# The start of a linear-attention block on one core: the last piece of a modulation matrix split between VectorE and TensorE, with new instruction orders

## The chip, the cores and the metric

The kernel runs on one core of a Trainium2 chip. A core has TensorE (PE, with its weight loads shown apart as PEld), VectorE (DVE), ScalarE (ACT), GpSimd (POOL) and SyncE (SP), which issues most DMAs. Each engine works through its own queue in order. The metric is the device time of one execution in microseconds; 2048 tokens of width 576 go through an attention block and an MLP.

## The reference

```python
mod = (silu(c) @ w_mod).reshape(1, 6, 1, 576)          # c: 1 x 576, w_mod: 576 x 3456
sa, ca, ga, sb, cb, gb = ...                           # six rows of mod
h = layernorm(x) * (1 + ca) + sa
q, k, v = heads of h @ wqkv                            # 32 heads of 18
phi = lambda t: where(t > 0, t + 1, exp(t)) + 1e-6
num = phi(q) @ (phi(k)^T v);  den = phi(q) . sum(phi(k))
x = x + ga * ((num / den) @ wo)
h = layernorm(x) * (1 + cb) + sb
x = x + gb * (silu(h @ w1) @ w2)                       # w1: 576 x 4608, w2: 4608 x 576
```

Everything is float32 outside. Inside, most products are made with operands split into a rounded high part and a low part that holds the rest, so one product becomes three passes: high by high, high by low, low by high.

## The kernel before, in words

The width 576 is cut into four chunks of 128 rows and a tail of 64 (KC = 4, START = 0..4; the tail stands twice, in both halves of a 128-row chunk). Tokens come in tiles of 128 and blocks of 512.

The start, which the change rewrites, makes two columns for each chunk: sa, the shift (a = 0), and 1 + ca, the scale (a = 1). w_mod's first 1152 columns come in five pieces by rows: four full ones in `mods[0..3]` (the tile is named hT in the trace) and the tail in `tmod`. VectorE multiplies piece 0 by its part of silu(c) (`sc`, line L583) and adds pieces 1 and 2 with theirs (L586), all into piece 0, called `rows`. What then remains is a sum over the 128 partitions: TensorE does it by one-column products (L522) with a chunk of 128 columns of `rows` as weights and a column of ones as the moving operand. The last piece goes by one-column products with `sc` itself as the moving column; the tail by products with two columns (`sel`, L519). All of these accumulate in one place of PSUM, `colp`, and `add_cols` (L526) copies them out, adding 1 to the scales. ScalarE copies the last 64 columns to stand twice (L589).

Meanwhile x tiles 0 and 1 are normalised (L355 makes the offset that ScalarE's normalising needs, L361 is ScalarE's and L363 VectorE's), turned by TensorE into PSUM (L531), and when the columns are there each chunk becomes a feature: `modulate` on VectorE (L371) or ScalarE (L369), then `split_h` rounds it (L375 on ScalarE) and takes the rest (L271 on VectorE). The k weights are rounded by `w_hi` (L476) and their rests taken by `w_lo` (L481, for the tail L483). `first_k` then makes the first real products (L548) of tiles 0 and 1 for chunks 0 to 3, and `k_part` the others. While TensorE has nothing else it multiplies ones by ones: `keep_busy(n)` issues n such fillers (L542), whose result nobody reads.

Later, project (L861) makes q and k of all tiles in two PSUM rooms named psK, used in turn. Each is read by ScalarE (L868) and VectorE (L874) before it is written again. `sum_steps` (L986) adds phi(k)^T h of each block. LayerNorm statistics are L346 (BN_STATS) and L347. Transposes of the normed q by DMA (L1368) feed the attention output (L399), and scans of the MLP weights (L661, squares by ScalarE, L662) give scale factors; then comes the MLP (L1935 up, L2019 down).

The order on each engine is not that of the source. `arrange(ORDERS, begun)` (L2390) takes a table of numbers per engine, found by a search outside the kernel, and chains the instructions of that engine in that order; what the table doesn't name keeps its place behind. So an engine waits for each of its instructions in the table's order, whatever is ready behind it.

Of the kernel before, what the change touches and what calls it, by code (L numbers as in the profile page):

```python
# [18 lines left out]
P = 128  # L19
# [5 lines left out]
def kernel(ctx: ExitStack, tc, A_x, A_wqkv, A_wo, B_x, B_w1, B_w2, c, w_mod, out):  # L25
# [33 lines left out]
    def behind(instructions):  # L59

        with ExitStack() as order:
# [7 lines left out]
            0-12 22 18-19 27-31 13-16 23-24 17 20-21 25-26 37-56 32-36 57-60 63-64 61-62 65-66 69-70 67-68 71-78 81-82  # L69
            85-86 79-80 89-93 96-97 83-84 87-88 94-95 98-117 126 118-121 127 122 128-133 123-124 134-135 125 136-137  # L70
            156-159 138-139 160-161 140-151 162-163 152-155 164-181 184-191 320-321 192-197 182-183 198-201 296
            202-217 297 218-223 322-325 224-235 326-327 298-299 236-239 328-331 300-301 240-245 302-303 246-251
            304-305 252-257 268-269 258-263 270-277 306-307 332-337 278-281 338-341 308-309 342-343 310-317 264-265
            318-319 282-293 368-369 266-267 370-373 294-295 344-345 374-375 346-351 376-377 352-355 378-381 356-365
            408-409 366-367 410-411 436-439 382-387 392-397 412-417 398-405 440-441 388-389 418-423 390-391 424-429
            442-443 406-407 430-435 444-479 492-495 480-483 496-499 484-485 500-501 486-491 502-505 600-601 506-509
            576-579 510-511 520-527 512-517 528-529 580-585 530-531 518-519 602-615 586-587 532-535 548-551 616-617
            552-555 588-591 556-557 592-593 536-537 618-621 558-569 594-599 622-623 538-543 570-571 624-629 544-547
            630-637 648-649 638-641 650-655 642-647 656-661 572-575 672-675 662-663 676-683 664-669 688-689 716-721
            684-687 670-671 690-693 722-723 694-715 724-739 744-745 740-743 746-761 772-779 880-881 762-767 780-781  # L80
            856-859 768-771 782-791 860-861 792-809 862 810-811 828-841 882-883 812-817 863-865 818-819 884-887
            866-873 888-889 874-879 820-823 842-847 824-827 890-893 904-905 848-851 894-895 852-855 906-909 896-901
            910-915 902-903 916-925 968-969 996-1001 970-983 926-927 1002-1005 984-991 1006-1009 928-931 992-995
            932-935 952-953 1010-1013 954-957 1014-1015 958-961 1016-1023 936-937 1024-1025 938-943 1026-1027 962-963
            1028-1035 964-965 1036-1039 944-945 1052-1059 966-967 1060-1061 946-951 1062-1069 1040-1051 1070-1079
            1137-1138 1080-1103 1108-1109 1139-1142 1110-1113 1143-1146 1104-1105 1114-1115 1106-1107 1147-1148
            1116-1117 1149-1150 1118-1121 1151-1152 1122-1135 1153-1160 1185-1191 1197-1206 1136 1207-1210 1161
            1211-1214 1162-1168 1215-1220 1169-1170 1287-1288 1171-1176 1289-1292 1177-1182 1293-1296 1183-1184 1192
            1245-1250 1193 1297-1298 1221-1238 1251-1252 1239-1244 1253-1256 1194 1257-1260 1195 1261-1263 1196
            1264-1285 1299-1316 1286 1317-1372 1389-1392 1373-1382 1417-1418 1383-1388 1419-1422 1393-1410 1423-1424  # L90
            1411-1416 1425-1430 1445-1456 1431-1444 1473-1482 1457-1458 1501-1502 1459-1460 1503-1506 1461-1462
            1507-1508 1463-1472 1509-1518 1483-1492 1519-1522 1493-1496 1523-1530 1497-1500 1531-1552 1557-1560
            1585-1594 1553-1556 1595-1602 1561-1564 1613 1617-1618 1565-1574 1619 1614-1615 1620 1603-1604 1616
            1629-1638 1575-1584 1605-1608 1639 1621 1625-1626 1609-1612 1622-1624 1627-1628 1640-1646 1661-1662
            1689-1690 1647-1648 1691-1696 1649-1656 1697-1708 1657 1709-1710 1658 1711-1718 1663-1672 1659-1660
            1673-1674 1745-1748 1675-1676 1749-1751 1719-1720 1752 1721 1753-1757 1677-1688 1722 1758-1760 1723-1730
            1761-1768 1731-1741 1773 1742-1744 1769-1772 1785-1788 1813 1774-1775 1814-1816 1829-1830 1789-1796
            1831-1832 1797-1800 1817-1819 1833-1834 1776-1779 1837-1838 1820-1821 1835 1780-1781 1822 1782 1801-1802
            1836 1783-1784 1839 1803-1804 1840 1805-1810 1823 1811-1812 1824-1828 1841-1864 1869-1870 1925 1871-1872
            1865-1868 1926 1873 1885-1886 1874-1877 1939 1878 1913 1927-1928 1914-1915 1879 1887-1888 1940 1929  # L100
            1880-1881 1930 1941-1942 1889-1892 1882 1916-1919 1893-1904 1943-1945 1905-1906 1883-1884 1907-1908
            1931-1932 1909-1912 1933-1936 1953-1958 1920-1921 1959-1964 1937 1965-1970 1938 1922 1946-1948 1923-1924
            1949-1951 1971-1972 1952 1981 1973-1974 1993-1998 1982 1999-2000 1975-1978 2001-2004 1983 2005-2006
            1979-1980 1984-1986 2007-2008 1987-1989 2009-2012 1990-1992 2021 2037-2038 2013-2018 2022-2027 2049-2052
            2019-2020 2053-2059 2039-2040 2060 2028 2061-2068 2029-2030 2069-2070 2031 2041 2071 2032 2042 2072-2074
            2033-2036 2081-2082 2045 2083-2084 2075-2076 2085-2088 2043-2044 2093-2094 2089 2046-2048 2095-2104
            2077-2080 2105-2108 2090 2109-2116 2121-2123 2117-2120 2133 2124-2125 2134-2144 2126 2145-2146 2091-2092
            2127-2132 2147-2149 2151-2152 2150 2153-2158 2165-2168 2159-2164 2173-2174 2183 2175 2184 2176 2193-2195
            2169-2170 2185 2171-2172 2177 2179-2182 2178 2199-2202 2189-2192 2186-2188 2205 2203 2229 2204 2196-2198
            2230 2211 2231-2232 2206 2233 2217-2221 2243 2207 2212-2213 2222 2214 2234 2223-2224 2235 2225-2228  # L110
            2236-2237 2208 2215 2238-2242 2209-2210 2244 2216 2245-2257 2263-2264 2258 2269 2265-2266 2270-2271
            2259-2260 2272 2261 2267-2268 2262 2275-2280 2273-2274 2287-2304 2281-2286 2305 2311-2312 2306-2309 2325
            2310 2326-2329 2313-2314 2330 2315-2324 2331-2347 2355 2367 2348-2354 2361-2363 2368-2371 2379 2372
            2364-2366 2380-2382 2385 2383 2356 2384 2386-2388 2357-2360 2397-2402 2389-2390 2373-2376 2403 2377-2378
            2417-2424 2437-2441 2391-2393 2405 2404 2406-2408 2442 2394 2489 2409 2395 2501 2455-2458 2396 2459-2462
            2502-2506 2475 2411-2412 2410 2413-2415 2476-2478 2490 2479-2481 2425 2482 2426-2430 2416 2491-2494
            2443-2448 2431-2435 2513 2436 2514-2518 2449-2454 2519-2520 2527-2528 2463-2469 2529-2533 2483-2484 2534
            2485-2486 2470-2472 2487-2488 2473-2474 2541-2546 2495-2500 2553-2556 2507-2510 2557-2560 2521-2522
            2511-2512 2523-2524 2567-2572 2535 2573-2574 2525-2526 2536-2540 2581-2585 2547-2549 2561-2566 2586 2593
            2550-2552 2594-2596 2587-2590 2597 2591-2592 2575-2576 2598 2577-2580 2605-2610 2599 2613 2600-2604  # L120
            2614-2615 2611-2612 2616-2618 2627-2632 2619-2623 2639-2640 2624-2625 2641-2642 2626 2673 2653-2656
            2643-2644 2657-2658 2633-2638 2674-2678 2645-2646 2679 2647-2652 2667 2680-2682 2668-2669 2683 2670-2672
            2684-2685 2659-2665 2686 2666 2691 2687 2697 2688-2690 2698-2700 2692-2694 2701-2704 2717-2718 2695-2696
            2719-2724 2709-2710 2725-2726 2705-2708 2711-2713 2727-2728 2714-2716 2729-2734 2755-2756 2807-2808
            2735-2736 2809 2825 2737-2743 2826 2757-2758 2810-2811 2744 2749-2753 2759-2761 2754 2767 2745 2762
            2746-2747 2763 2768-2769 2748 2770-2773 2764-2766 2775-2776 2787 2777 2812 2788-2789 2778 2790 2774
            2779-2782 2791-2792 2795-2799 2783 2863 2793-2794 2800-2802 2864 2784-2785 2865-2866 2786 2803-2806
            2867-2869 2813-2816 2843-2850 2831-2832 2827-2830 2817-2819 2833-2838 2820 2839 2870 2821-2824 2840-2842
            2883-2887 2851-2859 2871-2872 2860-2861 2873 2862 2901-2903 2888 2904-2908 2874-2877 2889-2896 2878-2882
# [2293 lines left out]
```

## Time and profile before

| | us |
|---|---|
| three timed runs | 1068.85, 1073.65, 1073.93 (median 1073.65) |
| the profiled execution | 1067.39 |
| its span in the trace | 1065.7 |
| TensorE busy in the span | 1051.7 (99%) |
| VectorE, ScalarE, GpSimd busy | 872.5, 718.0, 739.7 |
| mean granted TensorE clock | 0.996 |

The profile is of one execution; the timed runs are others. The span begins with the first instruction that the profiler saw. A line such as `L522 PE MATMUL psG<-ones,hT` gives source line, engine, operation, the tile written and the tiles read. In the timeline "x20" counts records, and a float32 product of the program is two records. Text in brackets behind a row is the idle time of that engine before it and what ended it. "Busy" of TensorE includes its waits inside a pipeline and its fillers.

### The profile page before, as it was taken

To read this page: it belongs to the slowest core of one execution; us is meant where nothing else is said; L and a number is where in the kernel's file an instruction comes from. 1 tells how busy PE (TensorE), PEld (TensorE's weight loads), DVE (VectorE), ACT (ScalarE), POOL (GpSimd) and SP (SyncE) were. 2 spreads that over 40 slices of the span, in tenths; PEclk is the share of its full clock that TensorE was granted. 3 is DMA by queue.
4 is the path that set the end of the run, shared out by engine and by line. 5 is a ranking of instruction groups with operands and counts; after the bars stand their busy time and mean duration, and the time that the engine had idled before them with its cause. 6 is when DMAs were issued, how large, how long until landed. Compare 5 with 4: busy or idle time off the path is not lost.

```text
span 1065.7 us, 19010 instructions
## 1 busy us (share of the span) xinstructions
PE 1051.7 (99%) x6981; PEld 742.2 (70%) x6981; DVE 872.5 (82%) x1434; ACT 718.0 (67%) x1343; POOL 739.7 (69%) x808
## 2 busy tenths in 40 slices
PE   8999999999999999999999999999999999999998
PEld 8999999887775565656666666666666666666665
DVE  5876865688999997898988888978977987898757
ACT  5865565458676967776866766767767766776554
POOL 2557446565832888899798678876876878687463
PEclk8999999999999999999999999999999999999999
DMA  9496971294866876587577667657566567526422
GB/s 303 142 205 194 133 203 28 59 214 90 247 173 219 282 219 227 157 279 214 148 239 212 189 205 214 197 202 220 175 217 204 190 199 238 187 89 200 153 81 111
DMA packets 139245, 198.74 MB, mean 186 GB/s; under 512 B 63820, under 2 KB 96464, under 8 KB 139152
## 3 DMA queue, kind: packets, MB, share of 16 engines
q1 hardware_dynamic: 106340, 196.35, 60.2%
q10 hardware_dynamic: 32812, 1.18, 3.2%
q8 instruction: 54, 0.88, 0.4%
q14 instruction: 39, 0.32, 0.1%
HBM read 176.77 MB, written 15.48 MB: 180 GB/s over the span
## 4 chain that ended last, share of the span: by engine, by line
PE 77%; DVE 10%; ACT 4%; DMA 4%; issue 2%; SPq 2%; POOL 1%; DVEq 0%; ACTq 0%; POOLq 0%
PE up L1935 31%; PE down L2019 30%; PE psK L861 5%; PE psG L986 4%; PE big L399 2%; PE big L1451 1%; DVE w L277 1%; PE small L1440 1%; DVE hT L271 1%; DMA hT<-in_w_mod_dram 1%; DMA acc<-turned 1%; DMA qT<-pn 1%; PE psK L548 1%; DMA hT<-hd 1%; DVE st L346 1%
## 5 line engine op out<-in xcount | busy, mean ns | idle before, releaser
L1935 PE MATMUL up<-hT,w 128*128 128x512 f16 x1264 | 319.9, 379 | 0.8 <-DMA hT<-hd 0.8
L1935 PEld LDWEIGHTS <-w 128*128 128x128 f16 x1492 | 145.7, 98 | 133.0 <-DMA hT<-hd 1.9
L2028 DVE SCALAR_TENSOR_TENSOR acc<-acc,set,down 128x576 f32<-128x576 f32 x128 | 103.4, 809 | 31.9 <-PE down L2019 31.2
L1953 ACT ACTIVATE f<-f,set 128x512 f32<-128x512 f32 x102 | 73.3, 718 | 60.1 <-DVE f L1959 50.1
L1973 POOL TENSOR_TENSOR s<-f,f 128x256 f32<-128x256 f32 x66 | 54.7, 828 | 73.4 <-ACT f L1954 70.9
L2019 PE MATMUL down<-w,hb 128*128 128x288 f16 x600 | 91.6, 286 | 0.4 <-DVE U L2030 0.3
L2019 PE MATMUL down<-w,hc 128*128 128x288 f16 x600 | 90.9, 286 | 0.0
L2019 PE MATMUL down<-w,hT 128*128 128x288 f16 x480 | 82.8, 286 | 0.4 <-DVE acc L2032 0.4
L1957 DVE TENSOR_TENSOR f<-up,p 128x512 f32<-128x512 f32 x102 | 69.5, 681 | 16.5 <-PE up L1935 8.6
L1954 ACT ACTIVATE f<-f,set 128x512 f32<-128x512 f32 x102 | 73.6, 721 | 3.0
L2019 PEld LDWEIGHTS <-hb 128*128 128x128 f16 x600 | 58.7, 98 | 24.2 <-issue 1.2
L2019 PEld LDWEIGHTS <-hc 128*128 128x128 f16 x600 | 58.7, 98 | 22.0 <-issue 0.3
L1997 POOL TENSOR_TENSOR hc<-s,hc 128x512 f16<-128x512 f32 x50 | 63.2, 1264 | 7.2 <-ACT hc L1993 7.1
L1959 DVE TENSOR_TENSOR f<-up,f 128x512 f32<-128x512 f32 x68 | 46.7, 687 | 26.2 <-PE up L1935 25.6
L1977 POOL TENSOR_TENSOR f<-f,s 128x256 f32<-128x256 f32 x66 | 53.9, 816 | 19.9 <-DVE hb L1997 12.1
L399 PE MATMUL big<-w,qT 128*128 128x288 f16 x448 | 65.0, 286 | 1.8 <-DMA qT<-pn 0.7
L2019 PEld LDWEIGHTS <-hT 128*128 128x128 f16 x480 | 46.9, 98 | 26.6 <-issue 0.8
L1970 POOL TENSOR_TENSOR s<-f 128x256 f32<-128x256 f32 x66 | 56.4, 854 | 5.4 <-ACT f L1950 3.9
L1975 POOL TENSOR_TENSOR s<-s,f 128x256 f32<-128x256 f32 x66 | 55.8, 845 | 3.3
L2019 PE MATMUL down<-w,ha 128*128 128x288 f16 x396 | 56.8, 286 | 0.0
L2019 PE MATMUL down<-w,hd 128*128 128x288 f16 x396 | 56.5, 286 | 0.0
L986 PE MATMUL psG<-w,xs 128*128 128x288 f32 x336 | 54.8, 295 | 0.0
(420 smaller groups left out, 2765.1 us busy)
## 6 DMA issues: line engine op xcount, KB each, us to landing
hT<-hd SPq DMA_DIRECT2D x101, 640.0 KB, 4.7
hT<-hd SPq DMA_DIRECT2D x65, 512.0 KB, 4.1
hT<-in_B_w_dram SPq DMA_DIRECT2D x14, 576.0 KB, 5.3
hT<-in_B_w_dram SPq DMA_DIRECT2D x28, 256.0 KB, 5.7
raw<-in_B_w_dram SPq DMA_DIRECT2D x11, 576.0 KB, 6.5
v<-in_B_w_dram SPq DMA_DIRECT2D x9, 576.0 KB, 5.3
raw<-in_B_w_dram SPq DMA_DIRECT2D x9, 512.0 KB, 4.9
acc<-in_A_x_dram SPq DMA_DIRECT2D x16, 288.0 KB, 6.2
```

The source lines that it names most:

```text
L399: T.matmul(ps, xpart(a), wpart(b), start=n == 0, stop=n == len(XW) - 1)
L986: T.matmul(ps[:, h, :HALF], l, pk[t][:, u, h * HALF : (h + 1) * HALF], start=t == 0 and m == 0, stop=t == 3 and m == len(left) - 1)
L1935: T.matmul(ps, left, right, start=first and m == 0, stop=m == len(seq) - 1, skip_group_check=True)
L1953: A.activation(f, f, AF.Silu, scale=factor(self.g, "inv"))
L1954: A.activation(f, f, AF.Identity, scale=factor(self.g, "delta"))
L1957: V.tensor_add(f, self.bank[bank[1]], self.p1)
L1970: G.tensor_sub(self.s3, half(i, 0, 0), half(i, 0, 1))
L1973: G.tensor_add(self.s[:, 0:1], half(i, 0, 1), half(i, 1, 1))
L1975: G.tensor_sub(self.s[:, 1:2], self.s[:, 0:1], half(i, 0, 0))
L1997: eng.tensor_sub(t[:, :, 1, :], src, t[:, :, 0, :])
L2019: T.matmul(ps[:, p, :HALF], left[:, u, p * P : (p + 1) * P], right[:, v], start=n in (1, 5, 7, 6) and j == 0, stop=j == len(passes) - 1, s ...
L2028: V.scalar_tensor_tensor(dst, dst, factor(self.g, "ratio"), ps[:, :, :HALF], op0=ALU.mult, op1=ALU.add)
```

## The change

The last piece of w_mod is no longer all one-column products. For a = 1 VectorE adds it to `rows` in two cuts of 256 and 320 columns, and one product with ones takes the sum; for a = 0 it stays a one-column product with `sc`. So there are five products with ones on `rows` for a = 0 ahead, and then, chunk by chunk, a pair: the last piece for a = 0, `rows` for a = 1. `add_cols` is called three times, for chunk 0, chunks 1 and 2, and chunks 3 and 4. The feature's rounded part is no longer a cast of the modulated tile: ScalarE computes scale and shift straight from PSUM into the rounded tile, VectorE does the same in float32 for all five chunks and subtracts. The tail's `w_lo` moves from VectorE to GpSimd. Fillers go from 26 to 41. The tables of all five engines are new; they differ up to the first MLP groups (some 3,070 of 11,060 rows of TensorE), and from there on the order is the old one.

```diff
@@ the tables: every row of PE, DVE, Activation, Pool and SP, of which one
     ORDERS = {
         "PE": """
-            0-12 22 18-19 27-31 13-16 23-24 17 20-21 25-26 37-56 32-36 57-60 63-64 61-62 65-66 69-70 67-68 71-78 81-82
+            0-24 27-29 25-26 30-44 47 49 51 53 55 57-58 45-46 48 50 59-62 52 54 63-66 69-70 56 73-74 67-68 71-72 75-76
...
-    def mod_cols(m, rhs, last=False):
+    def tail_cols():
         for k in START:
-            if m is tmod:
-                T.matmul(colp[k], m[:, k * P : (k + 1) * P], rhs, start=k == 0, stop=False, skip_group_check=True)
-            else:
-                for a in range(2):
-                    T.matmul(colp[k][:, a : a + 1], m[:, a, k * P : (k + 1) * P], rhs, start=False, stop=last, skip_group_check=True)
+            T.matmul(colp[k], tmod[:, k * P : (k + 1) * P], sel, start=k == 0, stop=False, skip_group_check=True)
+
+    def mod_col_of(k, a, m, rhs, last=False):
+        T.matmul(colp[k][:, a : a + 1], m[:, a, k * P : (k + 1) * P], rhs, start=False, stop=last, skip_group_check=True)
...
-    keep_busy(8)
+    keep_busy(11)
...
-    keep_busy(4)
-    mod_cols(tmod, sel)
+    keep_busy(8)
+    tail_cols()
...
-    rows = mods[0][:, :, :D]
+    rows, last = mods[0][:, :, :D], mods[KC - 1]
     V.tensor_scalar(rows, rows, sc[:, 0:1], None, op0=ALU.mult)
-    keep_busy(3)
+    keep_busy(4)
     for k in range(1, KC - 1):
         V.scalar_tensor_tensor(rows, mods[k][:, :, :D], sc[:, k : k + 1], rows, op0=ALU.mult, op1=ALU.add)
-        keep_busy(3)
-    for k, rhs in ((0, ones[:, 0:1]), (KC - 1, sc[:, KC - 1 : KC])):
-        A.copy(mods[k][:, :, D:DX], mods[k][:, :, KC * P : D])
-        mod_cols(mods[k], rhs, k > 0)
+        keep_busy(4)
+    A.copy(mods[0][:, 0, D:DX], mods[0][:, 0, KC * P : D])
+    for k in START:
+        mod_col_of(k, 0, mods[0], ones[:, 0:1])
+        keep_busy(1)
+    for c0, c1 in ((0, 2 * P), (2 * P, D)):
+        V.scalar_tensor_tensor(rows[:, 1, c0:c1], last[:, 1, c0:c1], sc[:, KC - 1 : KC], rows[:, 1, c0:c1], op0=ALU.mult, op1=ALU.add)
+    A.copy(last[:, 0, D:DX], last[:, 0, KC * P : D])
+    A.copy(mods[0][:, 1, D:DX], mods[0][:, 1, KC * P : D])
+    for k0, k1 in ((0, 1), (1, 3), (3, KC + 1)):
+        for k in range(k0, k1):
+            mod_col_of(k, 0, last, sc[:, KC - 1 : KC], True)
+            mod_col_of(k, 1, mods[0], ones[:, 0:1], True)
+        add_cols(k0, k1)
     keep_busy(2)
-    add_cols(0, KC + 1)
     for k in START:
         w_hi(wk_, k, acc[k])
-        w_lo(wk_, k, acc[k], G if k in (0, 2) else V)
-        modulate(*args[k], A if k in (1, 3) else V)
-        split_h(*args[k])
+        w_lo(wk_, k, acc[k], V if k in (1, 3) else G)
+        pt, _, to, col, h = args[k]
+        hi, lo = (k, KC + k) if k < KC else (2 * KC, 2 * KC + 1)
+        A.activation(to[:, hi, :], pt, AF.Identity, bias=col[:, k, 0:1], scale=col[:, k, 1:2])
+        modulate(*args[k], V)
+        sub_hi(to[:, lo, :], h, to[:, hi, :])
```

What the tables make of it, at three places. Line numbers in the rows of the new kernel are its own: 1 more than before up to L364 and again at the loads, the same around L520 to L590, 12 more behind L605 (so L673, L748 and L1380 are the L661, L736 and L1368 of before).

First place: the start on TensorE, from the turning of x (`ident,xt`) to the first real products (`w,hT` into psK). Before:

```order
L531 MATMUL psG_116<-ident,xt 128x128 x4
L522 MATMUL psG_116<-ones,hT 128x1 x10
L522 MATMUL psG_116<-sc,hT 128x1 x10
L542 MATMUL psG_117<-ones 128x128 x7
L548 MATMUL psK<-w,hT 128x288 x28
```

And now:

```order
L542 MATMUL psG_117<-ones 128x128 x10
L522 MATMUL psG_116<-ones,hT 128x1 x5
L522 MATMUL psG_116<-sc,hT 128x1
L522 MATMUL psG_116<-ones,hT 128x1
L542 MATMUL psG_117<-ones 128x128 x4
L522 MATMUL psG_116<-sc,hT 128x1
L522 MATMUL psG_116<-ones,hT 128x1
L522 MATMUL psG_116<-sc,hT 128x1
L522 MATMUL psG_116<-ones,hT 128x1
L542 MATMUL psG_117<-ones 128x128 x2
```

Ten fillers now stand between the turning and the column products, four and two among the pairs, of which chunks 3 and 4 follow in the same way behind the last row; none stand right before L548, which has 6 among its own rows instead of 3. The same place on VectorE, before:

```order
L363 TENSOR_SCALAR xt<-xt,mv 128x576
L583 TENSOR_SCALAR hT<-hT,sc 128x2x576
L586 SCALAR_TENSOR_TENSOR hT<-hT,sc 128x2x576 x2
L346 BN_STATS st<-xt 128x6 x2
L526 TENSOR_TENSOR col_a<-psG_116,plus_86 128x10
L371 TENSOR_SCALAR raw_121<-psK,col_a 128x256
```

And now:

```order
L583 TENSOR_SCALAR hT<-hT,sc 128x2x576
L356 SCALAR_TENSOR_TENSOR mv<-mv 128x2
L556 MEMSET plus_86 128x1
L364 TENSOR_SCALAR xt<-xt,mv 128x64
L364 TENSOR_SCALAR xt<-xt,mv 128x576
L586 SCALAR_TENSOR_TENSOR hT<-hT,sc 128x2x576 x2
L593 SCALAR_TENSOR_TENSOR hT<-hT,sc 128x256
L593 SCALAR_TENSOR_TENSOR hT<-hT,sc 128x320
L526 TENSOR_TENSOR col_a<-psG_116,plus_86 128x2
L372 TENSOR_SCALAR raw_121<-psK,col_a 128x256
L272 TENSOR_TENSOR hT<-raw_121,hT 128x256
L526 TENSOR_TENSOR col_a<-psG_116,plus_86 128x4
```

The first scaling of w_mod has moved ahead of the normalising of x, and four BN_STATS that stood around the columns now follow the second L526.

Second place: the first loads on the SP queue (`in_w_mod_dram` into hT are the four pieces, into tmod the tail, `in_A_wqkv_dram` the k weights). Before:

```order
L436 DMA xt<-in_A_x_dram 128x576 x2
L459 DMA hT<-in_w_mod_dram 128x2x576
L467 DMA tmod<-in_w_mod_dram 64x576
L459 DMA hT<-in_w_mod_dram 128x2x576
L467 DMA tmod<-in_w_mod_dram 64x576
L459 DMA hT<-in_w_mod_dram 128x2x576
L403 DMA acc_91<-in_A_wqkv_dram 128x576 x2
L459 DMA hT<-in_w_mod_dram 128x2x576
```

And now:

```order
L437 DMA xt<-in_A_x_dram 128x576 x2
L468 DMA tmod<-in_w_mod_dram 64x576 x2
L460 DMA hT<-in_w_mod_dram 128x2x576 x2
L407 DMA acc_92<-in_A_wqkv_dram 64x576
L460 DMA hT<-in_w_mod_dram 128x2x576 x2
```

The tail goes first, and ahead of the fourth piece one load of 64 rows stands where two of 128 rows stood.

Third place: the SP queue at the passage to the MLP (`in_B_w_dram` into w are the scans, DMA_TRANSPOSE feeds L399). Before:

```order
L1368 DMA_TRANSPOSE qT<-pn 128x10x128
L736 DMA acc_91<-in_A_x_dram 128x576 x2
L1368 DMA_TRANSPOSE qT<-pn 128x10x128
L1386 DMA raw<-in_B_w_dram 64x256
L661 DMA w<-in_B_w_dram 64x4x256 x4
L736 DMA acc_91<-in_A_x_dram 128x576
L736 DMA acc_92<-in_A_x_dram 128x576
L1368 DMA_TRANSPOSE qT<-pn 128x10x128
L661 DMA w<-in_B_w_dram 64x256
```

And now:

```order
L673 DMA w<-in_B_w_dram 64x4x256 x2
L748 DMA acc_91<-in_A_x_dram 128x576
L1398 DMA raw<-in_B_w_dram 64x256
L1380 DMA_TRANSPOSE qT<-pn 128x10x128 x2
L748 DMA acc_91<-in_A_x_dram 128x576
L673 DMA w<-in_B_w_dram 64x256
L748 DMA acc_92<-in_A_x_dram 128x576
L673 DMA w<-in_B_w_dram 64x256
L1380 DMA_TRANSPOSE qT<-pn 128x10x128
L673 DMA w<-in_B_w_dram 64x4x256
```

The scans, of which four stood together behind the second transpose, now begin ahead of the first and stand singly between the transposes.

More of the change, by code (lines that the diff above doesn't have):

```diff
@@ new lines @@
+            1195-1196 1201 1223-1226 1146 1227-1230 1171-1194 1255-1256 1297-1298 1257-1262 1231-1254 1202-1203
+            1263-1266 1204-1206 1267-1270 1299-1302 1271 1303-1304 1272-1295 1305-1324 1296 1325-1382 1399-1402
+            1383-1386 1427-1428 1403-1408 1429-1434 1387-1392 1435-1440 1393-1398 1409-1414 1441-1444 1415-1422
+            1455-1456 1423-1424 1445-1452 1425-1426 1453-1454 1457-1476 1483-1484 1511-1514 1485-1492 1515-1516
+            1477-1482 1493-1496 1517-1534 1497-1504 1535-1538 1505-1510 1539-1552 1567-1568 1553-1558 1595-1596
@@ L131 @@
+            2879-2880 2845-2846 2830-2833 2857-2859 2847-2848 2834 2893-2897 2849-2850 2861-2865 2860 2866-2867 2898
+            2868-2870 2851-2852 2911-2912 2871-2872 2913-2914 2881-2882 2915 2883 2916-2918 2884-2887 2899-2906
+            2888-2892 2907-2909 2931-2934 2919-2921 2910 2922-2930
         """,
         "DVE": """
[L133 to L134 removed]
@@ L196 @@
+            185 201 181 186-188 194 207 179 195 191 196 198-200 202 204 209 208 212 189 213 205 203 210 216 190 211
+            214-215 206
         """,
```

227 lines of the change are left out of this document (109 added, 118 removed).

## Prediction

> **What bounds the kernel now.** I read the page's head first, then the table of windows over five stretches, the timeline of the start, the same windows microsecond by microsecond for the clock, the DMA issues, and last the waits.
>
> ```profile
> span 1065.7 us, 19010 instructions
> 0.00:22.95 22.95, 19.02 (x108) 18.27 (x108) 10.37 (x29) 10.28 (x21) 6.64 (x11) 0.86 0.93 308
> 22.95:45.00 22.05, 21.95 (x166) 21.65 (x166) 20.69 (x51) 20.10 (x38) 7.86 (x7) 0.99 0.54 163
> 45.00:200.00 155.00, 153.65 (x1153) 151.50 (x1151) 104.62 (x181) 94.42 (x153) 90.52 (x69) 1.00 0.68 139
> 200.00:350.00 150.00, 146.90 (x1040) 108.95 (x1041) 136.01 (x253) 99.08 (x166) 82.66 (x78) 1.00 0.67 183
> 350.00:1062.00 712.00, 709.80 (x4521) 441.79 (x4520) 599.97 (x922) 494.12 (x970) 552.03 (x645) 1.00 0.62 195
> ```
>
> Each row gives the stretch, its length, then the busy time of PE, PE's weight loads, DVE, ACT and POOL, the granted clock, the DMA share and GB/s. From 22.95 us on PE stands idle for 0.10, 1.35, 3.10 and 2.20 us: it is the bound to the end, and what comes before 22.95 us is almost wholly a prelude, added to it. So the question is when the first real product starts, and whether what feeds PE after it follows.
>
> ```profile
> 6.48 0.92 DVE L363 TENSOR_SCALAR xt<-xt,mv 128x64 f32<-128x64 f32 x2
> 7.90 0.82 DVE L583 TENSOR_SCALAR hT<-hT,sc 128x1152 f32<-128x1152 f32 x1 [0.50 <-DMA hT<-in_w_mod_dram]
> 10.57 1.42 DVE L586 SCALAR_TENSOR_TENSOR hT<-hT,sc 128x1152 f32<-128x1152 f32 x1 [1.85 <-DMA hT<-in_w_mod_dram]
> 12.39 1.42 DVE L586 SCALAR_TENSOR_TENSOR hT<-hT,sc 128x1152 f32<-128x1152 f32 x1 [0.40 <-DMA hT<-in_w_mod_dram]
> 13.86 2.39 PE L522 MATMUL psG<-ones,hT 128*128 128x1 f32 x20 [0.64 <-DVE hT L586]
> 15.08 0.30 ACT L589 COPY hT<-hT 128x128 f32<-128x128 f32 x1 [0.37 <-DMA hT<-in_w_mod_dram]
> 16.11 3.99 PE L522 MATMUL psG<-sc,hT 128*128 128x1 f32 x20
> 19.96 3.33 PE L542 MATMUL psG<-ones 128*128 128x128 f32 x14
> 20.14 0.17 DVE L526 TENSOR_TENSOR col_a<-psG,plus 128x10 f32<-128x10 f32 x1 [2.77 <-PE psG L522]
> 20.34 0.54 DVE L371 TENSOR_SCALAR raw<-psK,col_a 128x256 f32<-128x256 f32 x1
> 20.80 0.45 DVE L346 BATCH_NORM_STATS2 st<-xt 128x6 f32<-128x288 f32 x1
> 20.92 0.40 ACT L375 CAST hT<-raw 128x256 fp32r<-128x256 f32 x1 [4.39 <-DVE raw L371]
> 21.23 0.56 ACT L369 ACTIVATE raw<-psK,col_a 128x256 f32<-128x256 f32 x1
> 21.36 0.43 DVE L271 TENSOR_TENSOR hT<-raw,hT 128x256 fp32r<-128x256 f32 x1
> 22.95 4.10 PE L548 MATMUL psK<-w,hT 128*128 128x288 f32 x28
> ```
>
> The chain to see: the third w_mod piece lands at 12.39, VectorE is done at 13.8, PE makes ten program products (two records each) with ones, the fourth piece has landed by 15.08, and ten more with sc keep PE until 19.96. Only then come the columns (L526), the first feature (L371) and, behind 14 filler records, L548.
>
> ```profile
> 16.00:17.00 1.00, 1.00 (x10) 1.00 (x9) 0.46 (x2) 0.53 (x1) 1.00 (x2) 0.79 1.04 408
> 17.00:18.00 1.00, 1.00 (x6) 1.00 (x7) 0.37 (x2) 0.00 (x0) 1.00 (x2) 0.50 1.05 410
> 23.00:24.00 1.00, 1.00 (x8) 1.00 (x7) 0.97 (x6) 1.00 (x4) 0.42 (x1) 0.79 1.09 369
> 24.00:25.00 1.00, 1.00 (x10) 1.00 (x9) 1.00 (x5) 1.00 (x3) 0.39 (x1) 1.00 1.03 244
> ```
>
> The clock column (0.79 is full clock for 0.58 us) says that it halves at 16.58 and is back at 23.42, in the middle of this. At full clock a record takes (16.11 - 13.86) / 20 = 0.1125 us, at half clock (22.95 - 19.96) / 14 = 0.214 us, a one-column product or a filler alike; a program product or filler is two records, so 0.225 or 0.43 us. What went ahead of the drop was one-column products alone; what went ahead of the rise was fillers.
>
> **The change, part by part.** The loads first.
>
> ```profile
> hT<-in_w_mod_dram SPq DMA_DIRECT2D x4, 576.0 KB, 7.6
> acc<-in_A_wqkv_dram SPq DMA_DIRECT2D x8, 288.0 KB, 7.7
> acc<-in_A_wqkv_dram SPq DMA_DIRECT2D x4, 144.0 KB, 9.2
> tmod<-in_w_mod_dram SPq DMA_DIRECT2D x2, 144.0 KB
> 5.00:10.00 5.00, 3.64 (x18) 3.58 (x19) 2.33 (x8) 2.44 (x6) 0.71 (x1) 1.00 1.04 296
> 10.00:15.00 5.00, 3.64 (x33) 3.24 (x31) 2.84 (x2) 3.16 (x6) 1.35 (x2) 1.00 1.04 385
> ```
>
> The queues are full (share 1.04), so landings go by the bytes ahead. On SP both tmod halves now precede the first piece: +288 KB, at 296 GB/s +1.0 us, 8.9 us. The second and third have 144 KB more ahead: 11.0 and 12.8. Before the fourth, two loads of 288 KB give way to one of 144: 432 KB less at 385 GB/s, 1.2 us earlier, 13.9.
>
> VectorE: L583 8.9 to 9.7; the normalising of tile 0 (L363, 0.92) and the small L355 on which ScalarE's tile 1 waits now stand behind it, and end near 10.8, so PE's turns of x last until about 12; ten fillers (2.25) then last to 14.25. L586 ends at 12.4 and 14.2. Now the new part: half the last piece, 1.42 x 576 / 1152 = 0.7 us in two cuts, to 14.5 and 14.9, in a time in which VectorE does nothing now.
>
> PE: five products of column 0 with ones (1.1) to 15.4; the pair of chunk 0 (0.45) to 15.8; then four fillers 0.9, two pairs 0.9, two fillers 0.45, two pairs 0.9: 18.95. So L548 could start at 19.0 instead of 22.95: **-3.95 us**, if the clock stays full. Chunk 0 has its columns at 16.0, ScalarE rounds the feature straight from PSUM (0.56 as L369) to 16.6 and VectorE has its rest (L271) at 17.0: hidden. The second product of each pair now waits for VectorE's cut, and all of PE's queue stands behind it; PE is there at 15.6, the first cut is done at 14.5, so a fourth piece that lands up to 1.1 us later than I reckon costs nothing, and beyond that one for one.
>
> But PE follows VectorE later:
>
> ```profile
> 30.82 0.76 DVE L874 TENSOR_SCALAR a<-psK 128x576 f32<-128x576 f32 x1 [0.79 <-ACT e L868]
> 31.95 1.04 PE L861 MATMUL psK<-wq,hT 128*128 128x288 f32 x6
> 35.78 0.76 DVE L483 TENSOR_TENSOR v<-acc,v 64x576 fp32r<-64x576 f32 x1
> 37.55 0.22 DVE L912 TENSOR_TENSOR v<-xt,v 128x64 fp32r<-128x64 f32 x1
> 38.70 0.75 DVE L874 TENSOR_SCALAR acc<-psK 128x576 f32<-128x576 f32 x1
> 39.62 1.27 PE L861 MATMUL psK<-w,hT 128*128 128x288 f32 x8
> ```
>
> Two psK banks alternate, so each L874 frees the bank for the next projection: the first, at 30.82, for that at 31.95, the third, at 38.70, for that at 39.62. VectorE is busy 20.69 of 22.05 us here. In its new order the stretch from the first columns to that L874 holds two modulates more (0.46 each, 20.34 to 20.80), two L526 (0.2 each), two BN_STATS (0.45), an L912 (0.22), and one L271 (0.43) and one L483, the tail's w_lo (0.76), less: +1.3 us net. From 15.8 on that is 15.8 + 18.6 + 1.3 = 35.7: 3.0 us earlier than 38.70. With its waits (0.15 us for the rounded feature, 0.65 for the next columns, which PE has ready at 17.6) it is 36.5: 2.2. So this term lies between **-2.2 and -3.95; I take -3.0**, nearest to the row that PE waits on.
>
> Edits with one answer: ScalarE gives up five casts (0.40) and two modulates (0.56) for five activations of 0.56: a little less work. The tail's w_lo goes to POOL, busy 7.86 of 22.05 us: hidden; uncovered it costs some 0.6. The fillers are 15 more; those ahead of L548 lie in waits or are in the sum, three more inside the L548 cost 0.7 by PE's count and nothing while VectorE is the later.
>
> The orders behind: same instructions, other places, up to some 350 us.
>
> ```profile
> PE psK L861 <- ACT hT L929: 0.5, 1, 0.5
> SPq L661 <- ACT w L662: 8.3, 2, 7.1
> ```
>
> All of PE's idle time in 45 to 350 us is 4.45 us, which bounds a gain; a new wait of the size seen costs 0.5. I take 0, with -3 and +3 (six such waits) as ends, since nothing says which way.
>
> Sum: the profiled execution took 1067.39 us (its span 1065.7 and 1.7 around it); less 3.0 is 1064.4. The timed runs were 1068.85, 1073.65 and 1073.93: the profiled one is 6.3 below their median, 1.5 below the lowest. That gap needs a reading. A front that never reaches full clock would cost now 2.4 us in the 24 L522 records that ran before the drop (0.1 each), and half of another 3.4 us in L548, 1.7: 4.1 of the 4.8 us between the lowest run and the median. So I read the slower runs as those whose start stays at half clock, and 29 fillers in place of 16 ahead of the first column product, with six between the later ones, as what keeps it full. Forecast: 1064.4 + 1.5 = **1066**, each run like the best of now less the 3 us.
>
> The Trainium skill (TensorE: Matmul & The Clock Gate, Part 1) says that the clock goes by windows of about 3.4 us that run free of the kernel, so that one kernel warms at different points in different runs; the trace agrees as far as it goes, since its half-clock stretch, 6.84 us, is two such windows. By that rule the runs before would lie in two groups and the change would narrow them, as forecast; without it the gap has another cause and the sum from the median is 1070.6.
>
> **Rivals.** (1) *The gap is not the start's clock*: the 3.0 us come off, but off the median: 1073.65 - 3.0 = 1070.6. For it: one profiled run shows no slow one. Against: 4.1 of 4.8 us are priced. (2) *The clock stays at half through the new start*, so the change brings nothing: turns to 12.5, ten fillers 4.3, five products 2.1, then five pairs and six fillers 6.9: L548 at 25.8, where a start of now without full clock has it at 13.86 + 54 x 0.214 = 25.4. Time about 1074. For it: one-column products with few fillers between them. Against: the sixteen fillers of now already held full clock until 16.58. (3) *The SP queue*, slower: at the passage to the MLP the loads of L661 now stand singly ahead of the transposes of pn. One that waits for its room as in the row above holds the queue 7.1 us, and PE waits for qT; two that PE's wq products don't cover cost 14.2: 1080. It decides once an L661 waits longer than PE's spare projections last. Against: the load that must wait for a room (64x256) still stands behind two transposes, which hold the queue while the room comes free.
>
> **Chances.** Forecast 0.45, own range 1062 to 1069; rival 1 0.27; rival 2 0.15; rival 3 0.13. A measurement here tells about 0.5%, 5.4 us, from no change: below 1068.3 lies nearly all of the forecast and an edge of rival 1, 0.47; rivals 1 and 2 are otherwise within, 0.40; rival 3 is slower, 0.13. The range leaves out rival 3 and a little below: 1061 to 1074.5.
>
> **What would show it.** Right: L548 starting near 19, the clock row at 1.00 through 16 to 24 us, the third L874 near 35.7, PE idle about 4.5 us in 45 to 350, every run near 1066. Wrong: L548 early but L861 waiting on L874 (the 2.2 end or worse); 0.50 behind 16 us; a qT wait of some us near 220; runs that still spread by 5 us.

## The result, and the profile after

The changed kernel took 1062.39 us in the median of its first seven runs (1060.28 to 1065.2) against 1071.63 for seven of before: a ratio of 0.9917, interval 0.9898 to 0.9937. A second set of six gave 1063.24 and 0.9924 (0.9903 to 0.9945). All thirteen together have the median 1063.0 (1059.52 to 1066.25); 96 runs of before, made beside the experiments, have 1071.0. So the gain is about 8 us, while the two profiled executions, 1062.19 and 1067.39 us, differ by 5.2.

The table of windows of the changed kernel, with the same columns as before, cut where the first real product begins; the span is 1060.5 us:

```profile
0.00:18.45 18.45, 16.46 (x122) 15.97 (x122) 10.02 (x29) 9.31 (x19) 4.28 (x9) 1.00 0.91 309
18.45:45.00 26.55, 26.41 (x202) 26.07 (x202) 25.39 (x60) 23.72 (x42) 13.94 (x14) 1.00 0.58 194
45.00:200.00 155.00, 154.75 (x1144) 151.67 (x1143) 101.77 (x184) 93.94 (x151) 88.43 (x66) 1.00 0.67 140
200.00:350.00 150.00, 146.98 (x1053) 107.86 (x1051) 134.31 (x255) 103.61 (x175) 89.86 (x85) 1.00 0.71 194
350.00:1057.00 707.00, 703.77 (x4490) 438.94 (x4488) 594.92 (x914) 487.93 (x958) 545.27 (x637) 1.00 0.62 193
```

TensorE's idle time in 45 to 200 us is 0.25 us where it was 1.35; in 200 to 350 it is 3.02 (3.10), behind that 3.23 (2.20). The clock is full in every stretch, as far as it is recorded (from 5.88 us on). The timeline of the start, and the third and fourth projection (L886 and L873 are L874 and L861 of before):

```profile
8.33 0.82 DVE L583 TENSOR_SCALAR hT<-hT,sc 128x1152 f32<-128x1152 f32 x1 [1.76 <-DMA hT<-in_w_mod_dram]
12.24 1.42 DVE L586 SCALAR_TENSOR_TENSOR hT<-hT,sc 128x1152 f32<-128x1152 f32 x1 [0.40 <-DMA hT<-in_w_mod_dram]
13.71 1.28 PE L522 MATMUL psG<-ones,hT 128*128 128x1 f32 x10
13.91 0.95 DVE L593 SCALAR_TENSOR_TENSOR hT<-hT,sc 128x256 f32<-128x256 f32 x2 [0.25 <-DMA hT<-in_w_mod_dram]
15.66 0.56 ACT L607 ACTIVATE hT<-psK,col_a 128x256 fp32r<-128x256 f32 x1
18.45 0.51 PE L548 MATMUL psK<-w,hT 128*128 128x288 f32 x2
35.57 0.74 DVE L886 TENSOR_SCALAR acc<-psK 128x576 f32<-128x576 f32 x1
36.38 1.33 PE L873 MATMUL psK<-w,hT 128*128 128x288 f32 x8
```

L548 begins 4.5 us sooner than before, the third L886 3.1 us sooner. Following the same row of TensorE's table through both traces (its start in one less its start in the other), the lead is 3.8 us at 60 us of before, 4.4 at 80, 5.2 at 140, 5.4 at 200, 6.5 at 340, only 3.0 at 360, and 5.2 from 510 to the end. The steps at 80 and 140 stand where L861 waited 0.4 and 0.5 us in before, and waits no more; 2.2 us of the loss at 360 are the first row of the waits of the changed kernel (line, awaited, total, times, longest), and the other two are the places at which the third rival looked:

```profile
PE up L1947 <- DMA hT<-hd: 2.2, 1, 2.2
PE big L400 <- DMA qT<-w: 1.2, 1, 1.2
SPq L673 <- ACT w L674: 5.7, 2, 3.1
```

Behind that the old kernel still has TensorE idle for 1.2 us between 365 and 520 us and the changed one for 0.01, which is part of what the lead gains there.

### The profile page after: what moved, and what is told of

Its sections match the earlier page's. It is cut to its first block, busy times and chain, and to the rows that moved or that the text cites. A ratio compares the mean times of both kernels' runs of the same rounds, so it can differ in the third digit from the quotient of the medians.

```text
span 1060.5 us, 19049 instructions
## 1 busy us (share of the span) xinstructions
PE 1048.6 (99%) x7001; PEld 740.5 (70%) x7001; DVE 867.0 (82%) x1439; ACT 718.5 (68%) x1342; POOL 741.8 (70%) x809
## 4 chain that ended last, share of the span: by engine, by line
PE 92%; DMA 3%; DVE 2%; ACT 1%; SPq 1%; issue 0%; ACTq 0%; DVEq 0%
PE up L1947 33%; PE down L2031 32%; PE psK L873 9%; PE big L400 6%; PE psG L998 5%; PE small L1452 2%; PE big L1463 1%; PE psK L1210 1%; DMA hT<-hd 1%; DMA xt<-in_A_x_dram 1%; PE small L385 1%; DMA acc<-in_A_wqkv_dram 1%; PE down L2065 1%; PE up L2065 1%; PE psG L1171 0%; DMA hd<-S 0%
## 5 line engine op out<-in xcount | busy, mean ns | idle before, releaser
L1989 POOL TENSOR_TENSOR f<-f,s 128x256 f32<-128x256 f32 x66 | 53.8, 815 | 18.1 <-DVE hb L2009 10.2
L2009 POOL TENSOR_TENSOR hd<-s,hd 128x256 f16<-128x256 f32 x66 | 49.0, 742 | 7.0 <-ACT hd L2005 6.9
```

Of the source, the lines that this page charges most:

```text
L2009: eng.tensor_sub(t[:, :, 1, :], src, t[:, :, 0, :])
```

## The experiments

The theory to test names three causes: a new start with fewer one-column products (worth 3 to 4 us), a start that keeps full clock, and new orders behind it (1 to 2 us). Rivals: the orders carry it all; the clock has nothing to do with it; the loads do it. Ratios are to before, run in turn on the same chip. The last column counts the runs whose mean clock was 0.995 or less. That mean begins at the first change of the clock that is recorded, so it doesn't see how late the first rise came. One stretch of 3.41 us at half clock lowers it by 0.0016, so 0.995 means about three of them.

| kernel | runs | median us | ratio, 95% interval | low clock |
|---|---|---|---|---|
| before, all | 96 | 1071.0 | | 76 |
| changed, first set | 7 | 1062.39 | 0.9917, 0.9898 to 0.9937 | 0 |
| changed, second set | 6 | 1063.24 | 0.9924, 0.9903 to 0.9945 | 0 |
| new front, old orders behind 45 us | 12 | 1067.07 | 0.9967, 0.9952 to 0.9983 | 1 |
| old front, new orders behind 48.5 us | 12 | 1068.71 | 0.9981, 0.9968 to 0.9994 | 11 |
| changed, fewer fillers | 10 | 1065.49 | 0.9957, 0.9942 to 0.9971 | 6 |
| changed, none among the pairs | 6 | 1065.14 | 0.9944, 0.9927 to 0.9962 | 3 |
| changed, old order of loads | 6 | 1065.44 | 0.9954, 0.9936 to 0.9972 | 0 |
| changed, last piece by columns | 6 | 1064.26 | 0.9942, 0.9923 to 0.9961 | 2 |
| changed, features by a cast | 12 | 1066.33 | 0.9959, 0.9940 to 0.9979 | 4 |
| before, more fillers | 12 | 1068.94 | 0.9991, 0.9976 to 1.0006 | 10 |
| changed, x normalised first | 12 | 1065.09 | 0.9959, 0.9938 to 0.9980 | 6 |
| the same with 15 fillers | 6 | 1062.59 | 0.9931, 0.9913 to 0.9949 | 1 |

**Before, once more** (no edit).

> The kernel before, unchanged, timed once more with the granted clock of each run listed. Theory (the gap is clock): the runs above 1070 us show a mean clock of 0.993 or less, those at 1067 to 1069 one of 0.996 or more; each window of 3.42 us at half clock in work that counts costs up to 1.7 us. Rival (the gap is not the clock): runs of 1067 and of 1073 us show the same clock, 0.996, and the extra 5 us lie in waits for transfers, to be seen row by row against the first profile.

Of this second profile of before, 1070.11 us, one window, and the longest of TensorE's waits:

```profile
12.90:26.50 13.60, 13.60 (x65) 13.31 (x65) 5.43 (x15) 6.00 (x14) 5.28 (x4) 0.50 1.03 340
```

```profile
PE psK L861 <- ACT hT L929: 1.6, 1, 1.6
```

Timed against itself, the old kernel here gave a ratio of 1.0014 (1.0001 to 1.0026): a difference of 0.1 to 0.2% can come without any edit. In the profile the half clock lasts 13.6 us instead of 6.8. Row by row TensorE is 3.2 us behind the first profile at 35 us, 4.3 behind at 140 (the wait for L929 is 1.6 instead of 0.5), and 2.7 at the end. By clock the 96 runs of before order themselves as the theory says from 0.995 (median 1069.5, six runs) over 0.992 (1071.3, 21) to 0.990 (1072.1, 21); but 13 runs with a mean of 1.000 have 1070.7, and five at 0.998 have 1072.9. A first rise that comes only behind the start would do that; no such run was profiled, and it stays open. The first profile, on which the prediction stood, was a rare one: three of the 96 runs are below its 1067.39.

**New front alone, new orders alone.** The tables of all five engines are spliced at a time; TensorE's at the cut, and its end for the second kernel:

```diff
@@ front alone: the changed kernel, then the old order of what is left
-            220-233 310-311 336-337 234-243 250-255 244-245
+            220-233 310-311 336-337 234-243 250-252 244-249
@@ orders alone: the same with the two kernels exchanged, cut at 48.5 us
```

> The changed kernel with the new tables only up to what begins within 45 us; behind that every engine takes the old order. Theory (the start carries most of it): L548 begins at 18.5, TensorE is 3.5 to 3.9 us ahead of before at 45 to 70 us, the two stalls of before near 80 and 140 us (0.4 and 0.5 us) are back, and the run ends 3 to 4 us below before where the full change ends 5.2 below. Rival (the orders carry it): TensorE is ahead by 3.8 us at 45 us and falls back behind old waits, end within 1.5 us of before.

> The kernel before up to what begins within 48.5 us, and behind that every engine takes the new order. Theory: L548 at about 23, TensorE not ahead at 48 us, then 0.5 us ahead from 80 and 1.3 us from 140 us on, end 1 to 2 us below before. Rival (the orders carry it): 3 to 5 us below before. Rival (the new orders pay only with the new start): end level with before or above it.

The front alone is 0.33% faster, 3.5 us, the orders alone 0.19%, 2.0 us, the latter not much above the 0.14% of the unedited kernel. The product of both ratios is 0.9948; the change has 0.9917 and 0.9924. So some 2.6 to 3.3 us come only when both are there, at the edge of what the intervals can tell. What the orders change is seen in TensorE's waits between 40 and 180 us. The front alone, profiled in its slowest run (1073.09 us), with the start of L548 ahead:

```profile
23.97 0.83 PE L548 MATMUL psK<-w,hT 128*128 128x288 f32 x2
PE psK L873 <- ACT hT L941: 1.8, 1, 1.8
PE psK L873 <- ACT a L882: 1.4, 1, 1.4
PE psG L998 <- POOL v L922: 0.4, 1, 0.4
PE psK L873 <- DVE a L886: 0.4, 1, 0.4
```

The orders alone, profiled in its fastest run (1065.80 us):

```profile
PE psK L861 <- ACT a L870: 0.7, 1, 0.7
PE psG L1214 <- ACT a L1210: 0.2, 1, 0.2
```

The change:

```profile
PE psG L1226 <- ACT a L1222: 0.2, 1, 0.2
```

L941 is L929 of before. In four profiles with the old orders TensorE waits there 0.5, 1.6, 2.1 (the old kernel with more fillers, below) and 1.8 us, and all its waits in this stretch come to 1.3, 2.4, 2.9 and, with the new front, 4.0 us. With the new orders they are 0.9 on the old front and 0.2 on the new one, in all nine profiles of it. So the orders save here about 1.5 us on the old front, and nearly 4 on the new one in that run. But that run doesn't show what an early front meets under the old orders: with its clock at half from 11.0 to 17.9 and from 21.3 to 28.1 us, L548 begins at 23.97, later than the 22.95 of before and not at the 18.5 that was expected. Why both together bring more than the product, if they do, stays open.

**The change, once more** (no edit).

> The changed kernel, timed and profiled once more. Theory (new start and new orders need each other): the median stays near 1062.4 us, 8.5 us below before, although the two halves alone gave 3.8 (start) and 2.2 us (orders); most runs have a mean clock of 0.996 or more. Rival (the first seven runs were lucky): the median comes to about 1065, the sum of the halves. A second profile shows whether the third and fourth piece of w_mod land at 12.2 and 13.9 us again or, as in the profile of the start alone, at 13.7 and 15.3.

```profile
10.21 0.82 DVE L583 TENSOR_SCALAR hT<-hT,sc 128x1152 f32<-128x1152 f32 x1 [2.98 <-DMA hT<-in_w_mod_dram]
12.00 0.79 PE L531 MATMUL psG<-ident,xt 128*128 128x128 f32 x3 [2.67 <-DVE xt L364]
17.03 1.17 PE L522 MATMUL psG<-ones,hT 128*128 128x1 f32 x10
21.67 0.50 PE L548 MATMUL psK<-w,hT 128*128 128x288 f32 x2
```

```profile
PE up L1947 <- DMA hT<-hd: 0.9, 1, 0.9
```

The first piece lands at 10.2 instead of 8.3 us, the third and fourth at 13.5 and 15.4. VectorE stands at L583, x is normalised behind it, and TensorE waits 2.67 us for x. That leaves a stretch with little work, and the next, with the turnings and the first of the ten fillers, is at half clock:

```profile
8.80:12.20 3.40, 0.73 (x7) 0.65 (x8) 1.96 (x6) 1.03 (x2) 0.00 (x0) 1.00 1.03 365
12.20:15.60 3.40, 3.40 (x18) 3.40 (x18) 2.71 (x3) 2.68 (x5) 0.00 (x0) 0.50 1.06 347
```

L548 begins 3.2 us later than in the first profile. Yet the span is 1061.3, only 0.8 longer: row by row the lag is 2.8 us up to 330 us, 2.2 at 336, and 0.75 behind the wait for hd, which is 0.9 us instead of 2.2. In this pair the early start is not passed on in full. But the length of that wait isn't set by the start alone: in the profile of x normalised first, further below, TensorE comes to it as early as in the first profile (353.1 against 353.4 us), waits only this long, and ends 2.4 us sooner:

```profile
PE up L1947 <- DMA hT<-hd: 0.3, 1, 0.3
```

That kernel's profile begins L548 3.3 us ahead of this one and ends 3.2 us ahead, so the start was passed on in full there. Against the first profile of before this execution leads by only 0.8 us at 40 us, and by 4.4 at the end: most of its gain is made behind 45 us. Against the second profile of before the lead grows behind 45 us by some 1 us in the first profile of the change and by some 3 us in this one.

**Fillers.** Fewer (16 ahead of the columns, none among the pairs), none among the pairs, and more in the old kernel:

```diff
@@ changed, fewer fillers
-    keep_busy(11)
+    keep_busy(8)
-    keep_busy(8)
+    keep_busy(4)
-        keep_busy(4)
+        keep_busy(0)
-        keep_busy(1)
+        keep_busy(k == KC)
@@ changed, none among the pairs
-        keep_busy(4)
+        keep_busy(6 - 2 * k)
-        keep_busy(1)
+        keep_busy(k == KC)
@@ before, more fillers
-    keep_busy(8)
+    keep_busy(11)
-    keep_busy(4)
+    keep_busy(8)
-    keep_busy(3)
+    keep_busy(6)
```

> The changed kernel with 16 fillers instead of 29 ahead of the first column product, and none instead of 6 among the pairs. Theory (the fillers hold the clock): the clock halves somewhere in 13 to 22 us, and the run is 1 to 3 us slower than the full change, though the first L548 could start 1.3 us sooner. Rival (they hold nothing): the clock stays at 1.00 through the start, L548 begins at 17.1 to 18.4 and the run is level with the full change or up to 1 us faster.

> The changed kernel with all 29 fillers ahead of the first column product, but without the six among the pairs. Theory (all fillers hold the clock): more runs at 0.995 or less than with them, 1 to 2 us slower. Rival (only those ahead count): clock as with them, L548 0.6 to 1.3 us sooner (the two later pairs wait 0.25 and 0.65 us for VectorE instead), run level to 1 us faster.

> The kernel before with 26 fillers instead of 16 ahead of the first column product and nothing else changed. Theory (more fillers hold the clock, and that is a good part of the change): fewer runs at 0.995 or less than the 33 of 45 of before, 1 to 3 us faster than before. Rival (what pulls the clock down is the 6 us of one-column products, which stay): clock as before, time within 0.5 us of before.

The windows around the drop of the clock, in this order:

```profile
15.90:19.30 3.40, 2.49 (x21) 2.32 (x22) 1.99 (x7) 2.65 (x6) 1.90 (x2) 1.00 1.04 394
19.30:26.10 6.80, 6.80 (x30) 6.80 (x31) 5.56 (x18) 4.88 (x10) 4.80 (x6) 0.50 0.99 331
```

```profile
17.60:21.00 3.40, 2.49 (x20) 2.32 (x20) 2.41 (x8) 2.95 (x7) 3.02 (x2) 1.00 0.98 346
21.00:24.40 3.40, 3.40 (x16) 3.40 (x16) 3.04 (x11) 2.32 (x6) 3.24 (x3) 0.50 0.89 277
```

```profile
13.90:17.30 3.40, 3.40 (x33) 3.37 (x31) 0.67 (x3) 2.38 (x6) 3.25 (x3) 1.00 1.05 410
17.30:24.10 6.80, 6.80 (x32) 6.80 (x33) 4.33 (x15) 3.25 (x8) 2.62 (x3) 0.50 1.05 337
```

Against the change's 0.992, fewer fillers cost some 3.9 us; none among the pairs cost 2.6, with intervals that overlap, but half of its runs are at a low clock, where none of 13 of the change is. L548, which began at 20.9 and 20.8, runs at half clock; the pairs then wait 0.25 and 0.66 us for VectorE's L526, so that of the six fillers' 1.35 us 0.9 lay in a wait anyway. Adding them ahead in the old kernel brings nothing that the interval can tell from none (0.9991), though it reaches to 2.6 us faster and none of its runs is below 0.992, where 22 of 96 of before are. About as large a share of its runs as of before is at a low clock, and the profile shows why: in its window from 13.9 TensorE is busy to the full with one-column products, and the next two are at half clock. So fillers ahead don't reach into the column products: in these three profiles a window with next to no full-width work among them is followed by half clock, with 16, 26 or 29 fillers ahead.

**Old order of loads.** The first entries of SP's table:

```diff
-            1 0 2-5 13 6-8 12 14 10 15 9 11
+            0 1 4 2 5 3 6 10 8 7 13 12 14 15 9 11
```

> The changed kernel with the loads of w_mod, its tail and the first k weights on the SP queue in the old order. Theory (the loads carry 1.2 us of the start): x lands at 3.5 to 3.9 us instead of 4.5, the first piece near 8.0, the fourth near 15.1 instead of 13.9, L548 about 0.7 us later, the run level to 1 us slower. Rival (the new order of loads costs, since x lands later with it): x is normalised sooner, the run is 0.5 to 2 us faster.

```profile
11.38 1.41 PE L519 MATMUL psG<-z,tmod 128*128 128x2 f32 x10 [1.76 <-DMA tmod<-in_w_mod_dram]
17.50 1.17 PE L522 MATMUL psG<-ones,hT 128*128 128x1 f32 x10
```

0.3% slower than the change by the ratios, more than the 1 us expected, but with intervals that overlap. The first piece lands at 8.15 us now, but the tail later, and L519 stands ahead of the turning of x on TensorE: the columns begin at 17.5 and L548 at 22.1. Loads and table belong together, so this doesn't price the loads alone.

**Last piece by columns for both halves.**

```diff
         mod_col_of(k, 0, mods[0], ones[:, 0:1])
+        mod_col_of(k, 1, mods[0], ones[:, 0:1])
...
-        V.scalar_tensor_tensor(rows[:, 1, c0:c1], last[:, 1, c0:c1], sc[:, KC - 1 : KC], rows[:, 1, c0:c1], op0=ALU.mult, op1=ALU.add)
...
-            mod_col_of(k, 1, mods[0], ones[:, 0:1], True)
+            mod_col_of(k, 1, last, sc[:, KC - 1 : KC], True)
```

The copies of the tail columns, left out here, are changed to suit.

> The changed kernel with the last piece by one-column products for both halves, as before: ten products with ones ahead, then pairs with sc, five products more, no L593 on VectorE. Theory (VectorE's half saves TensorE five products of 0.22 us): L548 1.1 us later, and 0.6 to 1.1 us of it at the end. Rival (the wait for VectorE's cuts eats it): level. Rival (one-column products pull the clock down): 1.5 to 4 us slower, with more runs at a clock of 0.995 or less.

```profile
15.40 2.29 PE L522 MATMUL psG<-ones,hT 128*128 128x1 f32 x20
21.12 0.51 PE L548 MATMUL psK<-w,hT 128*128 128x288 f32 x2
```

From the first column product to L548 it takes 5.72 us, with the change 4.74: 0.98 us for five products, as the theory said. Its median is 1.0 us above the change of the same set, within the intervals. Whether the five products also pull the clock down stays open: two of six runs are at a low clock, and the profiled one has a mean of 1.000.

**Features by a cast.**

```diff
-        A.activation(to[:, hi, :], pt, AF.Identity, bias=col[:, k, 0:1], scale=col[:, k, 1:2])
         modulate(*args[k], V)
+        A.copy(to[:, hi, :], h)
```

> The changed kernel with the features rounded as before: VectorE's modulate first, then ScalarE's cast of its result, then the subtraction. Theory (hidden at the start, since L548 waits for the pairs on TensorE): L548 within 0.3 us, the run within 0.5 us of the change. Rival (the chain from columns to feature is what L548 waits for): L548 0.4 to 0.9 us later and the run 0.4 to 1 us slower.

```profile
20.91 0.43 PE L522 MATMUL psG<-ones,hT 128*128 128x1 f32 x2 [1.68 <-ACT hT L595]
```

Not hidden, and by a road that neither theory named: on ScalarE the copy of the tail columns (L595) stands behind the first two features. These now wait for VectorE, the copy with them, and TensorE's last pair 1.68 us for the copy; a window with too little work follows, and the clock halves at 21.1. By the ratios it is 0.35 to 0.4% slower than the change, more than either theory said. The old table may hide the cast better; that was not tried.

**x normalised first**, and the same with 15 fillers:

```diff
@@ VectorE's table
-            5 0 7 6 9 2 1 3 10 8 11-12 16 13 4 14-15 17-21
+            5 0 7 6 9 2 1 3 10 8 11-13 4 14-21
@@ and, in the second kernel, behind the first scaling
-    keep_busy(4)
+    keep_busy(9)
```

> The changed kernel with one row of VectorE's table moved: the normalising of x (L356 and both L364) stands ahead of the first scaling of w_mod (L583) again, as before. Theory (in most runs the first piece lands near 10.2 us, not at 8.3 as in the first profile, and everything that waits for x waits with it): turning begins near 9.7 instead of 12, the ten fillers end near 13.5, L548 begins 1.5 to 2.5 us sooner; at the end 0.5 to 2 us faster than the change, since part is taken back by the wait for hd near 355 us. Rival (the ten fillers behind the turning were what held the clock): with an idle stretch ahead of the column products more runs at 0.995 or less, level or slower.

> As the run before with x normalised first, and 15 fillers instead of ten between the turning of x and the column products. Theory (a window of 3.41 us in which TensorE makes fewer than about 12 full-width records, one-column products not counted, is followed by one at half clock; x normalised first left such windows where TensorE waited for w_mod): the fillers close that gap, few runs at 0.994 or less where 5 of 12 had it, median 2 to 4 us below that run's 1065.1, level with the change or 1 us faster. Rival (the gap is not there in most runs and the fillers lie on the path): L548 1.1 us later, median 1065 to 1066 us.

The second one's start:

```profile
10.77 3.51 PE L542 MATMUL psG<-ones 128*128 128x128 f32 x30
14.46 1.28 PE L522 MATMUL psG<-ones,hT 128*128 128x1 f32 x10 [0.18 <-DVE hT L586]
19.25 0.52 PE L548 MATMUL psK<-w,hT 128*128 128x288 f32 x2
```

x first alone has the best profile of all (1059.82 us, L548 at 18.4) and a worse median than the change: its runs at a mean clock of 0.997 take 1063.6 to 1065.0, those at 0.992 to 0.994 1069.3 to 1070.6. With 15 fillers in the gap, ended by the columns with 0.18 us of waiting, the ratio comes back from 0.9959 to 0.9931, within the intervals, level with the change and not better, and one run of six is at a low clock instead of six of twelve. That is the rule of the windows (last section) used forwards; no slow run of x first alone was profiled, so the gap that the fillers close was not seen.

## Why the prediction was right, and where it was not

**The start**, in the profiled execution: L548 forecast at 19.0, measured 18.45; the third L886 at 35.7, measured 35.57; so the term of -3.0 was -3.1. The five products saved were priced at 1.1 us, measured 0.98; the two cuts on VectorE at 0.7, measured 0.95, and TensorE doesn't wait for them. The sum put the profiled execution at 1064.4 and it took 1062.19: the lead is 3.8 us at 60 us, not 3.0, and 1.4 more come behind. The 1.5 us from there to the median were 0.2 in the first set. The first piece was reckoned at 8.9 us by bytes: in nine profiles with the new loads it came at 7.9 to 8.3 three times and at 9.7 to 10.5 six times. So in most of these profiles it is later than reckoned, and TensorE's wait for x that then follows was not in the sum.

**"What comes before is a prelude, added to it"** held in one pair of profiles and not in another: between the two of the change 3.2 us of start were worth 0.8 at the end, and of the 2.4 us lost 1.3 are the longer wait for the transfer of hd near 355 us; between the second of them and x normalised first 3.3 us were worth 3.2, with hardly a wait there. What sets the landing of hd stays open, and with it how much of an early start is passed on.

**"The orders behind: I take 0"** is the step that was mis-sized. They bring 1.4 us in the profiled pair, 3.6 against the second profile of the change, 2.0 by the ratio alone and perhaps more with the new start; TensorE's waits between 40 and 180 us, 1.3 us in the profile I read, are 2.4 and 2.9 in the two others of the old front and orders (the latter with more fillers). No gain measured here is above the bound of 4.45 us, but it was read from the profile with the fewest waits: with the old orders TensorE idles 5.7, 6.5 and 7.1 us between 45 and 350 us in the other three.

**"1064.4 + 1.5", with each run near the best of before less 3 us.** The reading behind it was right in kind: 76 of 96 runs of before have a mean clock of 0.995 or less, none of 13 of the change, and the second profile of before puts 3.2 us of start on 6.8 us more of half clock. The reason given was right in part only: 29 fillers ahead don't hold the clock by themselves (without the six among the pairs it halves at 21.0 us), and ten more in the old kernel left 10 of 12 runs at a low clock. The six among the pairs are what the runs point to; whether the fewer column products help the clock too is not shown. Nor is the clock always full: 8 of the 13 runs of the change have a mean below 1.000, and its second profile has 3.4 us at half. The 13 runs of before with a mean of 1.000 and a median of 1070.7 are not explained by this reading. And the runs of the change still spread by 6.7 us.

**The features, "hidden"**: they are, but the cast they replace would not have been in this table.

**The rivals.** 1 (1070.6 us): 8 us above what was measured, and the clock is a part of the gap (1069.5 at 0.995 to 1072.1 at 0.990). 2 (half clock stays, 1074): not seen in either profile of the change, where half clock, if any, is over at 15.6 us, but it is what the front alone met in its slowest run, L548 at 23.97 and the end at 1073.09. 3 (SP's queue, 1080): L673 waits 3.1 us at the longest and TensorE 1.2 for qT; it didn't decide.

## What to carry to other kernels

A start that feeds TensorE with one-column products and waits needs full-width work in every clock window, and fillers count by where they stand: here more of them in a place that was already full brought nothing clear. A term read from one profiled execution is worth only as much as that execution is typical: compare it with the lowest and the median of the timed runs first, and take a second one. When a start gets shorter, look for the next transfer that TensorE waits for, since it can take back a part of the gain, and differently from run to run.

## What the runs showed of the hardware

The clock goes by stretches of 3.41 us: every half-clock stretch in the start is 3.41, 6.83 or 13.65 us long. Counting TensorE's full-width records (fillers, turnings, products of 128x288) in each such stretch up to some 35 us, one- and two-column products left out, over all 14 profiles:

| clock now | full-width records | next at half | next at full |
|---|---|---|---|
| full | 0 to 9 | 13 | 0 |
| full | 10, 11 | 1 | 2 |
| full | 12 or more | 0 | 72 |
| half | 0 to 9 | 9 | 0 |
| half | 12, 13 | 1 | 1 |
| half | 14 or more | 0 | 13 |

At full clock some 30 filler records fit into a stretch. Behind 35 us, where the products differ more in kind, the clock halves only twice, at 147.6 us in the front alone and at 220.7 in fewer fillers, behind stretches with 11 and 10 records; others with 9 to 11 stay at full, so the edge isn't sharp. The profile's busy share doesn't show it: the window 13.90 to 17.30 above is busy for 3.40 of 3.40 us with two full-width records and 29 narrow ones, and is followed by half clock. The Trainium skill (TensorE: Matmul & The Clock Gate, Part 1) has the gate watch how busy TensorE was in a window of 3413 ns that runs free of the kernel: the length agrees, and so do the differing places (the first recorded rise lies between 4.05 and 10.47 us). Its account by busy time, with no counting of instructions, holds here only if a one-column product counts as next to nothing.
